# A convolution by two-stage transforms with two MLPs behind it: the last seven rows of the second transform sent from SBUF to SBUF, the inverse of two tiles in one go, two PSUM buffers shared by `ob` and `fk`

## The chip, the cores and the metric

The kernel runs on one core of one Trainium2 chip. The metric is device time in microseconds of one launch. Runs of the kernel before: 1381.61, 1382.43 and 1383.54 us; the median is 1382.43 us.

## What is computed

A gated long convolution over 12480 positions and 128 channels, then two MLPs of width 2048, all in float32:

```python
h_filt = (np.maximum(pos_emb @ w1, 0.0) @ w2) * np.exp(-0.01 * pos)[:, None]
u = x * v                                   # (1, 12480, 128)
y = np.fft.irfft(np.fft.rfft(u, n=L, axis=1) * np.fft.rfft(h_filt, n=L, axis=0), n=L, axis=1)[:, :S]   # L = 2 * S
x = x * y
h = x @ moe_w_in;  x = np.maximum(h, 0.0) ** 2 @ moe_w_out
h = x @ moe2_w_in; out = h / (1.0 + np.exp(-1.702 * h)) @ moe2_w_out
```

## The kernel before, in words

The transform of length 99 x 127 is made of matmuls. A first stage (L291 to L300) multiplies folded inputs by a 99-point table into `A`, 128 partitions by 99 rows (the row index is called k here) by (real, imaginary) by 128 channels.

**The second transform** (`stage_s2`, L322 to L423) goes through the rows in 50 pairs p. Per pair TensorE computes `xk` (spectrum of the signal, L365), every second pair `fk` (features of four filter rows, L342), every fourth pair `hk` (eight filter rows, L357), and two pairs later `ob` (L388), the way back. VectorE multiplies `xk` by the filter into `t` (L374) and subtracts two quarters into half of `P` (L378); GpSimd adds the other half (L377). ScalarE copies `fk`, `hk` and `ob` out of PSUM; the copy of `ob` goes back into `A` in place (L390). `xk` and `hk` have two PSUM buffers each, `fk` one and `ob` one (pool `obp`). Between these VectorE instructions the class `Weights` puts the conversion of MLP weights, which arrive as float64 words: one chunk of 512 columns is eight VectorE instructions on a 128x512 tile (L149, L151, L155, L157, L158, L160, L165, L169) and one ScalarE cast (L167), one step per tick and a tick per pair. Chunks start every six pairs, at pairs 3, 9, ... 45, so that now and then two of them step in the same pair.

Each group of four finished rows is stored from `A` to DRAM (`bd`, L398) and must come back with rows on partitions, because the inverse contracts over rows. For the first four output columns of each half, `load_first` (L490) loads rows 0 to 79, 80 to 87 and 88 to 98 from `bd` into the first columns of `A`; the last three rows are first stored by L394, and the load of the last eleven rows waits for that.

**The junction** between transform and MLPs, in program order: the last `ob` copy on VectorE (L390), the two stores (L394), the loads (L494), the late stores of the remaining columns (L497), `work.finish(EARLY)` with seven ticks of conversion on VectorE, eight combinations of `sums_first` (L455), seven spare matmuls on TensorE (L680), the inverse of tile 0 (20 matmul instructions into one PSUM tile `yps`, L553), the products `hi`, `y`, `lo` (L541 to L543), one more spare matmul, `work.finish()`, and then the MLP loop.

**The MLP loop** (L689 to L723) walks over units: unit (l, t, j) is layer l, tile t of 25 (492 to 502 positions), block j of 256 of the 2048 hidden columns. `unit_in` makes `hin` with six float32r matmuls (high and low parts, L595 to L597), ScalarE applies the activation (two instructions in layer 0), VectorE makes `gh` (`gate`, L636) and `gl` (`low`, L647), and four units later `unit_out` adds six matmuls into `acc`. From unit 40 on layers 0 and 1 alternate. In every tile of layer 0 the next tile is prepared: `load_b` brings two more columns of `bd` (`uv`), `combine_next` adds and subtracts them on VectorE into `b`, `front_y` does the inverse of the next tile on TensorE and multiplies by x on VectorE, `front_x` splits the result. `front_rest` (unit 9) makes the inverse of the two left-over segments into `yr`. The order on every engine is the program's order; nothing is reordered by a scheduler.

The PSUM pool `pms` behind `yps` has two buffers, used in turn:

```python
        pms = es.enter_context(tc.tile_pool(name="pms", bufs=2, space=PSUM, reuse_waits="tile"))
...
        def front_rest():
            ps = pms.tile([D, 512], FP32, tag="m", name="yps")
            inverse(ps, REST)
            nc.vector.tensor_copy(out=yr, in_=ps[:, 0:RESTW])
```

Of the kernel before, what the change touches and what calls it, by code (L numbers as in the profile page):

```python
# [14 lines left out]
ALU = mybir.AluOpType  # L15
# [37 lines left out]
EARLY = 7  # L53
# [19 lines left out]
def widths():  # L73
# [3 lines left out]
    for t, w in enumerate(whole):  # L77
        n = 0
        if t > 1 and left:
            n = min(left, -(-RESTW // (NTILE - 2)))  # L80
            n += (w + n) % 2
            n = left if t == NTILE - 1 else min(n, left)
        rest.append(n)
        left -= n
# [14 lines left out]
def conv_mlp_kernel(ctx: ExitStack, tc: tile.TileContext, xc, xt, vc, pt, w1, w2,  # L99
# [10 lines left out]
    bd = dram.tile([2, NJ, N1, 2, D], FP32, name="bd")  # L110
# [65 lines left out]
    class Weights:  # L176
# [18 lines left out]
        def finish(self, n=1 << 30):  # L195
            while n and (self.run or self.plan):
                self.tick(1 << 30)
                n -= 1
# [123 lines left out]
    def stage_s2(sp, mp, A, w2b, hooks, work):  # L322
# [3 lines left out]
        obp = tc.tile_pool(name="obp", bufs=1, space=PSUM, reuse_waits="tile")  # L326
# [5 lines left out]
        with kp as kp, obp as obp:  # L332
            def features(g):
# [5 lines left out]
                ps = kp.tile([128, FK, 128], FP32, tag="fk", name="fk", bufs=1)  # L339
# [42 lines left out]
            def back(p):  # L382
                n, m, P = pair(p), m_t.pop(p), P_t.pop(p)
                ob = (kp.tile([128, FK, D], FP32, tag="fk", name="ob", bufs=1).rearrange(
                    "p (k c) d -> p k c d", c=2) if p == NP - 2 else
                      obp.tile([128, 2, 2, D], FP32, tag="ob", name="ob"))
# [5 lines left out]
                if p == NP - 1:  # L392
                    for h, queue in ((0, nc.scalar), (1, nc.sync)):
                        queue.dma_start(out=bd[h, 0:JF1, k], in_=A[h * NJ:h * NJ + JF1, k])  # L394
                    for h in range(2):
                        late_h.append((h, k))
                elif k.stop - k.start == HK:
                    nc.scalar.dma_start(out=bd[:, :, k].rearrange("h j k c d -> (h j) k c d"), in_=A[:, k])  # L398
# [29 lines left out]
    def tile_parts(segs):  # L428

        at = 0  # L430
        for j, s, r, n in segs:
            yield j, s, r, n, at
            at += n
# [4 lines left out]
    b_t, x_t, pending = {}, {}, []  # L438
    loaded = [0]
# [6 lines left out]
    def sums(bp, slot):  # L446

        if slot < 2:
            return kept_half(slot)[0:N1].rearrange("p k q -> p (k q)").rearrange(
                "p (j s c d) -> p j s c d", j=JG, s=2, c=2)  # L450
        return bp.tile([N1, JG, 2, 2, D], FP32, tag="b", name="b", bufs=1)
# [16 lines left out]
    def pend(k):  # L468
        pending.extend((k, op) for op in (ALU.add, ALU.subtract))

    def combine_next(n):
        for i in range(min(n, len(pending))):
            combine_two(*pending.pop(0))

    def load_b(bp, t):


        last = max(p[0] for p in whole(t)) // JG
        for k in range(loaded[0], last + 1):
            uv = bp.tile([N1, 2, JG, 2, D], FP32, tag="uv", name="uv", bufs=2)  # L480
            for h in range(2):
                nc.sync.dma_start(out=uv[:, h], in_=bd[h, k * JG:(k + 1) * JG].rearrange("j k c d -> k j c d"))
            b = sums(bp, k % 3)
            b_t[k] = uv, b
            pend(k)
        loaded[0] = last + 1

    late_h = []

    def load_first(A, rows):  # L490


        for h in range(2):
            nc.sync.dma_start(out=A[rows, h * JF1:(h + 1) * JF1],  # L494
                              in_=bd[h, 0:JF1, rows].rearrange("j k c d -> k j c d"))
        for h, k in late_h:
            nc.sync.dma_start(out=bd[h, JF1:NJ, k], in_=A[h * NJ + JF1:(h + 1) * NJ, k])  # L497

    def sums_first(bp, A):
# [392 lines left out]
```

## Time and profile before

| | |
|---|---|
| median of three runs | 1382.43 us |
| the profiled execution | 1382.61 us, of which the span (first to last instruction) is 1380.8 us |
| TensorE busy | 1372.9 us, 99% of the span, 7754 matmul records |
| VectorE busy | 1109.2 us, 80% |
| ScalarE busy | 948.9 us, 69% |
| GpSimd busy | 61.0 us, 4% |
| chain that ended last, by engine | PE 92%, DVE 6%, ScalarE 1%, DMA 1%, issue 1% |
| granted TensorE clock | 0.999 |

PE is TensorE's matmuls, PEld its weight loads, DVE is VectorE, ACT ScalarE, POOL GpSimd, SP the SyncE queue. An instruction with float32 operands stands as two matmul records in the trace. A matmul record's busy time contains its drain, so the time from one start to the next tells the pace (about 0.22 us for 500 columns). The chain of waits goes back from the last instruction, at each step to what released it. In the stage tables the engines stand in the order PE, PEld, DVE, ACT, POOL, and the granted clock behind them is in parts of the full one.

### The profile page before, as it was taken

Reading aid. Unit: us, or ns where it says so; the run is one execution under the profiler, and the core shown is the slowest. Engines: PE = TensorE matmul, PEld = TensorE weight load, DVE = VectorE, ACT = ScalarE, POOL = GpSimd, SP = SyncE. Lnnn points to the kernel's source line nnn. Section 1 sums busy time; section 2 is a strip of 40 time slices with the busy share of each in tenths; the row PEclk is TensorE's granted clock in tenths of the full one; section 3 lists DMA queues with packets and bytes.
Section 4 is the critical chain, followed back from the end, with each engine's and each line's share of the span. In section 5 each row is a group of like instructions: output and inputs, shape, how many; then the busy total and the mean of one; then the engine's idle time right before and its main releaser. Section 6 shows DMA issues by size and latency. Waiting matters only on the chain.

```text
span 1380.8 us, 19037 instructions
## 1 busy us (share of the span) xinstructions
PE 1372.9 (99%) x7754; PEld 1139.9 (83%) x7754; DVE 1109.2 (80%) x1224; ACT 948.9 (69%) x1066; POOL 61.0 (4%) x61
## 2 busy tenths in 40 slices
PE   9999999999999999999999999999999999999998
PEld 8888886888888888888888888888888888888887
DVE  7559998888887787778777887778777887778887
ACT  2655554888776777667767777777777777777776
POOL 3013332000000000000000000000000000000000
PEclk9999999999999999999999999999999999999999
DMA  9968875111210000000000100001000000000000
GB/s 257 306 214 271 270 263 190 55 48 61 70 39 20 15 21 27 20 28 20 27 20 8 40 27 20 8 28 39 20 15 20 28 19 8 9 8 8 9 15 15
DMA packets 45843, 89.25 MB, mean 65 GB/s; under 512 B 4135, under 2 KB 30556, under 8 KB 44988
## 3 DMA queue, kind: packets, MB, share of 16 engines
q1 hardware_dynamic: 36744, 63.33, 15.4%
q10 hardware_dynamic: 9012, 24.70, 4.7%
q8 instruction: 61, 1.00, 0.3%
q14 instruction: 26, 0.21, 0.0%
HBM read 63.21 MB, written 24.81 MB: 64 GB/s over the span
## 4 chain that ended last, share of the span: by engine, by line
PE 92%; DVE 6%; issue 1%; ACT 1%; DMA 1%; SPq 0%; DVEq 0%; ACTq 0%
PE acc L595 13%; PE acc L596 13%; PE acc L597 13%; PE hin L595 13%; PE hin L596 13%; PE hin L597 13%; PE s L295 5%; PE yps L553 3%; DVE t L374 2%; PE ob L388 2%; PE xk L365 2%; PE hk L357 1%; PE fk L342 1%; DVE r L278 1%; DVE words L151 0%
## 5 line engine op out<-in xcount | busy, mean ns | idle before, releaser
L647 DVE TENSOR_TENSOR gl<-g,gh 128x1004 fp32r<-128x1004 f32 (+4 forms) x400 | 477.1, 1193 | 36.9 <-ACT gh L643 36.8
L623 ACT ACTIVATE g<-hin 128x1004 f32<-128x1004 f32 (+4 forms) x200 | 201.0, 1005 | 225.3 <-PE hin L597 219.2
L595 PE MATMUL acc<-gh,w 128*128 128x502 f32 (+4 forms) x800 | 313.8, 392 | 0.6 <-DVE lo L530 0.6
L596 PE MATMUL acc<-gl,w 128*128 128x502 f32 (+4 forms) x800 | 311.4, 389 | 0.6 <-DVE gl L647 0.6
L597 PE MATMUL acc<-gh,w 128*128 128x502 f32 (+4 forms) x800 | 311.4, 389 | 0.0
L595 PE MATMUL hin<-hi,w 128*128 128x502 f32 (+4 forms) x798 | 310.3, 389 | 0.3 <-ACT g L623 0.3
L596 PE MATMUL hin<-lo,w 128*128 128x502 f32 (+4 forms) x798 | 310.5, 389 | 0.0
L597 PE MATMUL hin<-hi,w 128*128 128x502 f32 (+4 forms) x798 | 309.4, 388 | 0.0
L638 DVE TENSOR_TENSOR g<-hin,g 128x1004 f32<-128x1004 f32 (+4 forms) x200 | 238.7, 1194 | 45.7 <-ACT g L628 45.5
L628 ACT ACTIVATE g<-hin 128x1004 f32<-128x1004 f32 (+4 forms) x200 | 200.1, 1000 | 70.4 <-PE hin L597 62.4
L636 DVE CAST gh<-g 128x1004 fp32r<-128x1004 f32 (+4 forms) x185 | 125.8, 680 | 137.1 <-ACT g L624 137.0
L624 ACT ACTIVATE g<-g 128x1004 f32<-128x1004 f32 (+4 forms) x200 | 208.0, 1040 | 6.3
L643 ACT CAST gh<-g 128x1004 fp32r<-128x1004 f32 (+4 forms) x200 | 202.7, 1013 | 0.3 <-DVE g L638 0.3
L595 PEld LDWEIGHTS acc<-gh,w 128*128 128x128 f32 x800 | 150.5, 188 | 33.9 <-DVE lo L530 1.0
L595 PEld LDWEIGHTS hin<-hi,w 128*128 128x128 f32 x798 | 150.2, 188 | 34.1 <-ACT g L623 3.5
L596 PEld LDWEIGHTS acc<-gl,w 128*128 128x128 f32 x800 | 150.9, 189 | 30.4 <-DVE gl L647 1.4
L597 PEld LDWEIGHTS acc<-gh,w 128*128 128x128 f32 x800 | 150.5, 188 | 30.4
L597 PEld LDWEIGHTS hin<-hi,w 128*128 128x128 f32 x798 | 150.4, 188 | 30.4
L596 PEld LDWEIGHTS hin<-lo,w 128*128 128x128 f32 x798 | 150.3, 188 | 30.2
L374 DVE TENSOR_TENSOR t<-xk,hc 128x1024 f32<-128x1024 f32 (+1 forms) x50 | 60.1, 1202 | 11.6 <-ACT hc L359 11.6
L377 POOL TENSOR_TENSOR P<-t 128x256 f32<-128x256 f32 (+1 forms) x50 | 48.4, 968 | 155.4 <-DVE t L374 141.0
L388 PE MATMUL ob<-P,m 128*128 128x256 f32 x198 | 53.0, 391 | 0.3 <-issue 0.3
(79 smaller groups left out, 954.2 us busy)
## 6 DMA issues: line engine op xcount, KB each, us to landing
m<-in_c_s_dram SPq DMA_DIRECT2D x49, 256.0 KB
bd<-A ACTq DMA_DIRECT2D x24, 512.0 KB
uv<-bd SPq DMA_DIRECT2D x62, 198.0 KB
x<-in_xc_dram SPq DMA_DIRECT2D x16, 384.0 KB
v<-in_vc_dram SPq DMA_DIRECT2D x16, 384.0 KB
Gs<-gd ACTq DMA_DIRECT2D x10, 512.0 KB
gd<-G SPq DMA_DIRECT2D x3, 1344.0 KB
pos<-in_pt_dram SPq DMA_DIRECT2D x16, 198.0 KB
```

The source lines that it names most:

```text
L374: nc.vector.tensor_tensor(out=t[:, 0:n], in0=xk[:, 0:n].unsqueeze(3).to_broadcast(full), in1=hc.unsqueeze(2).to_broadcast(full), op=ALU.mult)
L388: nc.tensor.matmul(out=ob[:, j], lhsT=m[:, j, 1, :], rhs=P[:, j])
L595: nc.tensor.matmul(out=out, lhsT=a, rhs=hl[0], start=first, stop=False)
L596: nc.tensor.matmul(out=out, lhsT=a, rhs=hl[1], start=False, stop=False)
L597: nc.tensor.matmul(out=out, lhsT=b, rhs=hl[0], start=False, stop=last)
L623: nc.scalar.activation(out=g, in_=ps, func=ACTF.Relu)
L624: nc.scalar.activation(out=g, in_=g, func=ACTF.Square)
L628: nc.scalar.activation(out=g, in_=ps, func=ACTF.Sigmoid, scale=1.702)
L636: nc.vector.tensor_copy(out=gh, in_=g)
L638: nc.vector.tensor_tensor(out=g, in0=ps, in1=g, op=ALU.mult)
L643: nc.scalar.copy(out=gh, in_=g)
L647: nc.vector.tensor_tensor(out=gl, in0=g, in1=gh.bitcast(FP32), op=ALU.subtract)
```

## The change

It has six parts.

1. `ob` and `fk` take turns on two PSUM buffers of one tag; the pool `obp` is gone. Weight chunks start every seven pairs instead of six, so the eighth and last chunk starts only after the transform.
2. Rows 92 to 98 (`DIRECT`) go from `A` to the load target straight, one DMA of eight pieces of 1 KB per row, on the queues of ScalarE (rows 92, 96, 98) and SP (93, 94, 95, 97). The target is now the ring of `kept` halves instead of `A`. Rows 0 to 83 and 84 to 91 still come over `bd`. `store_late` then stores rows 92 to 98 for all columns in one DMA of 896 KB. `bd` is laid out with the columns of the first tile in front (constant `c_s2` reordered to fit).
3. At the junction five ticks of conversion instead of seven stand in front of the combinations; six combinations instead of eight stand in front of the inverse (the other two behind `lo`). The remaining conversion steps go into units 2 and later, two ticks per unit. Spare matmuls: five in front of the inverse, none behind it.
4. Tile 0's inverse goes into two PSUM tiles: three segments (296 positions) in the first, two (196) in the second; `hi` and `y` are made in two pieces.
5. In every second tile `front_ps` makes the inverse of the next two tiles back to back; `front_rest` moves to unit 19 in front of such a pair. `uv` loads go into the `kept` halves, three `b` buffers.
6. The last unit is split in two halves on ScalarE and VectorE, with its second half of `hin` in a `pms` tile; the last output copy and store are split in two, on two queues.

```diff
-EARLY = 7
+EARLY = 5
+DIRECT = 92
...
+        def go_on(self, n, at=0):
+            for i in range(n):
+                self.tick(at)
...
-                ps = kp.tile([128, FK, 128], FP32, tag="fk", name="fk", bufs=1)
+                ps = kp.tile([128, FK, 128], FP32, tag="fk", name="fk")
...
-                ob = (kp.tile([128, FK, D], FP32, tag="fk", name="ob", bufs=1).rearrange(
-                    "p (k c) d -> p k c d", c=2) if p == NP - 2 else
-                      obp.tile([128, 2, 2, D], FP32, tag="ob", name="ob"))
+                ob = kp.tile([128, FK, D], FP32, tag="fk", name="ob").rearrange("p (k c) d -> p k c d", c=2)
...
+                for i in range(max(2 * p, DIRECT), 2 * p + n):
+                    (nc.scalar if i % 4 == 0 or i == N1 - 1 else nc.sync).dma_start(
+                        out=first_uv()[i:i + 1], in_=A[0:2 * JF1, i])
+                if k.stop - k.start == HK and k.start < DIRECT:
+                    nc.scalar.dma_start(out=bd[:, k], in_=A[:, k])
...
+    def store_late(A):
+        nc.sync.dma_start(out=bd[:, DIRECT:N1], in_=A[:, DIRECT:N1])
...
+        def first_y(ps, x):
...
+            h = inverse(ps[0], whole(0)[0:3])
+            inverse(ps[1], whole(0)[3:], h)
+            parts = (slice(0, h), ps[0]), (slice(h, w), ps[1])
+            for q, p in parts:
+                for o in hi, y:
+                    nc.vector.tensor_tensor(out=o[:, q], in0=p[:, q], in1=x[:, q], op=ALU.mult)
...
-        spare(7)
-        front_y(0)
-        spare(1)
-        work.finish()
+        spare(5)
+        front_first()
...
-        work = Weights([(2, 0), (3, 0), (2, 1), (3, 1)], 6, 12, 4)
+        rest, work = work, Weights([(2, 0), (3, 0), (2, 1), (3, 1)], 10, 10.67, 3)
         for n in range(len(seq) + LAG):
+            rest.go_on(2 * (n > 1), 1 << 30)
...
+                    if lead and j == at:
+                        if t == 2:
+                            front_rest()
+                        front_ps(t + 1)
+                        front_ps(t + 2)
+                        front_y(t + 1)
...
+                    elif lead and j == at + 1:
+                        front_y(t + 2)
...
-            work = Weights([(i, c) for c in range(NWC) for i in range(2)], 3, 6, 5)
+            work = Weights([(i, c) for c in range(NWC) for i in range(2)], 3, 7, 7)
...
+            store_late(A)
+            load_x(lp, 1)
+            work.go_on(EARLY)
+            sums_first(bp)
```

How the order moves on VectorE at the junction. `words` is conversion scratch, `w` the converted weights, `Gs` and `b` the sums, `yps` the inverse in PSUM, `xs` the x tile. Before:

```order
L390 COPY A<-ob 128x256 [waits PE_49]
L151 SCALAR_TENSOR_TENSOR words<-words 128x512
L155 TENSOR_SCALAR words<-words 128x512
L169 TENSOR_TENSOR w_958<-words,w_958 128x512 [waits Activation_49]
L157 TENSOR_SCALAR words<-words 128x512 [waits DVE_49]
L158 TENSOR_SCALAR words<-words 128x512 [waits DVE_49]
L160 SCALAR_TENSOR_TENSOR words<-words 128x512 [waits DVE_49]
L165 SCALAR_TENSOR_TENSOR words<-words 128x512 [waits DVE_49]
L455 TENSOR_TENSOR Gs<-A 99x2x128 [waits DMAHW5_49,DMAHW6_49,DMAHW4_49,DMAHW7_49,DMAHW3_49,DMAHW1_49]
L455 TENSOR_TENSOR Gs<-A 99x2x128 x7
L541 TENSOR_TENSOR hi_2304<-yps,xs 128x492 [waits DMAHW3_49,DMAHW2_49,DMAHW4_49,DMAHW0_49,DMAHW7_49,DVE_49,PE_49]
```

With the change (L-numbers are those of the new file: L152 is old L151, L170 old L169, L156 old L155, L158 old L157, L159 old L158, L161 old L160):

```order
L387 COPY A<-ob 128x256 [waits PE_49]
L152 SCALAR_TENSOR_TENSOR words<-words 128x512
L170 TENSOR_TENSOR w_958<-words,w_958 128x512
L156 TENSOR_SCALAR words<-words 128x512
L158 TENSOR_SCALAR words<-words 128x512 [waits DVE_49]
L159 TENSOR_SCALAR words<-words 128x512 [waits DVE_49]
L161 SCALAR_TENSOR_TENSOR words<-words 128x512 [waits DVE_49]
L463 TENSOR_TENSOR b<-Gs 99x2x128 [waits DMAHW4_49,DMAHW3_49,DMAHW5_49,DMAHW2_49,DMAHW6_49,DMAHW1_49,DMAHW7_49,DMAHW0_49,Pool_49]
L463 TENSOR_TENSOR b<-Gs 99x2x128 x3
L463 TENSOR_TENSOR b<-Gs 99x2x128 [waits Pool_49]
L463 TENSOR_TENSOR b<-Gs 99x2x128
L554 TENSOR_TENSOR hi_2270<-yps,xs 128x296 [waits PE_49]
L554 TENSOR_TENSOR y<-yps,xs 128x296 [waits DMAHW7_49,Activation_49]
```

Six conversion steps are left in front of the first combination, and `hi` starts on 296 positions.

On TensorE the inverse in unit 19, with the change, behind that unit's `hin`: `words` holds the sums of the left-over segments, `b` those of tiles 3 and 4.

```order
L568 MATMUL yps<-ci_61,words 64x98 x8
L568 MATMUL yps<-ci_61,b 64x99 x4
L568 MATMUL yps<-ci_61,b 64x98 x4
L568 MATMUL yps<-ci_61,b 64x99 x4
L568 MATMUL yps<-ci_61,b 64x98 x4
L568 MATMUL yps<-ci_61,b 64x99 x4
L568 MATMUL yps<-ci_61,b 64x98 [waits DVE_49]
L568 MATMUL yps<-ci_61,b 64x98 x3
```

The first row is `front_rest`, the next 20 instructions are tile 3's inverse, and the first of tile 4's waits for VectorE: the third use of two `pms` buffers waits for the copy `yr` of the first. What VectorE has in front of that copy in the program:

```order
L170 TENSOR_TENSOR w_2238<-words,w_2238 128x1024
L538 TENSOR_TENSOR lo_2779<-acc,hi_2778 128x494 [waits Activation_49]
L663 CAST gh<-g 128x2x492 [waits PE_49,Activation_49]
L679 TENSOR_TENSOR gl<-g,gh 128x2x492 [waits DVE_49]
L602 COPY yr<-yps 128x196 [waits PE_49]
```

The `gh` in the third row belongs to unit 19 itself, the `gl` to unit 18. In the kernel before, `front_rest` stood alone in unit 9 and the next `yps` came two units later.

## Rows read from the trace of the kernel before

**Rows 1.** Stage table: stretch, us, busy us (instructions) per engine, clock, DMA share, GB/s

```profile
111.30:133.20 21.90, 21.90 (x162) 19.09 (x162) 20.56 (x26) 11.41 (x17) 7.76 (x8) 1.00 0.78 265
133.20:211.60 78.40, 78.16 (x563) 66.21 (x562) 75.47 (x95) 40.61 (x61) 27.45 (x28) 1.00 0.81 267
235.80:262.00 26.20, 25.81 (x156) 20.77 (x156) 20.94 (x28) 22.49 (x24) 0.00 (x0) 1.00 0.33 106
1377.20:1380.80 3.60, 0.00 (x0) 0.00 (x0) 0.00 (x0) 0.50 (x1) 0.00 (x0) 0.80 0.18 70
```

**Rows 2.** Chain of waits in the second transform: start us, us, what

```profile
116.08 0.87 PE ob L388 x4
...
117.81 0.96 PE ob L388 x4
```

**Rows 3.** Timeline of VectorE in the second transform: start us, us, engine, line, operation

```profile
206.11 1.21 DVE L374 TENSOR_TENSOR t<-xk,hc 128x1024 f32<-128x1024 f32 x1
...
207.76 1.22 DVE L169 TENSOR_TENSOR w<-words,w 128x512 fp32r<-128x512 f32 x1
...
208.90 0.41 DVE L157 TENSOR_SCALAR words<-words 128x512 int32<-128x512 int32 x1
```

**Rows 4.** Chain of waits at the junction

```profile
227.28 1.92 DMA bd<-A
...
230.05 2.03 DMA bd<-A
```

**Rows 5.** Timeline of the junction

```profile
226.57 5.94 PE L680 MATMUL spare<-xs,ci 99*99 99x492 f32 x14
226.78 0.42 DVE L390 COPY A<-ob 128x256 f32<-128x256 f32 x1 [1.10 <-PE ob L388]
...
229.76 0.69 DVE L160 SCALAR_TENSOR_TENSOR words<-words 128x512 int32<-128x512 int32 x1
...
232.10 2.77 DVE L455 TENSOR_TENSOR Gs<-A 99x256 f32<-99x256 f32 x8 [0.92 <-DMA bd<-A]
...
232.58 2.40 PE L553 MATMUL yps<-ci,Gs 99*64 99x99 f32 x40
...
235.03 0.67 DVE L541 TENSOR_TENSOR hi<-yps,xs 128x492 fp32r<-128x492 f32 x1 [0.16 <-PE yps L553]
...
237.04 0.72 PE L613 MATMUL hin<-lo,w 128*128 128x492 f32 x2
```

**Rows 6.** VectorE groups by shape: count, busy us, mean ns

```profile
L566 DVE TENSOR_TENSOR y<-yps,xs 128x490 f32<-128x490 f32 x11 | 7.3, 661 | 0.0
...
L569 DVE TENSOR_TENSOR y<-yr,xs 128x10 f32<-128x10 f32 x14 | 2.2, 159 | 0.0
```

**Rows 7.** Timeline of TensorE around one tile's inverse in the MLP stage

```profile
421.80 0.39 PE L596 MATMUL hin<-lo,w 128*128 128x502 f32 x1
422.03 0.39 PE L597 MATMUL hin<-hi,w 128*128 128x502 f32 x1
...
424.53 0.39 PE L596 MATMUL acc<-gl,w 128*128 128x494 f32 x1
```

**Rows 8.** Chain of waits: the inverse matmuls of that tile, and the first matmuls of all

```profile
3.96 3.56 PE hp L273 x16
...
422.42 1.85 PE yps L553 x40
```

**Rows 9.** Timeline in unit 19 of the MLP stage

```profile
290.39 0.39 PE L597 MATMUL hin<-hi,w 128*128 128x502 f32 x1
...
294.44 1.20 DVE L647 TENSOR_TENSOR gl<-g,gh 128x1004 fp32r<-128x1004 f32 x1
```

**Rows 10.** Timeline of the last unit

```profile
1372.08 1.18 DVE L638 TENSOR_TENSOR g<-hin,g 128x980 f32<-128x980 f32 x1 [0.40 <-ACT g L628]
...
1374.40 0.49 PE L596 MATMUL acc<-gl,w 128*128 128x490 f32 x1 [0.56 <-DVE gl L647]
...
1377.13 0.57 ACT L666 COPY o<-acc 128x490 f32<-128x490 f32 x1 [2.83 <-PE acc L597]
```

More of the change, by code (lines that the diff above doesn't have):

```diff
@@ L78, in widths @@
         n = 0
-        if t > 1 and left:
-            n = min(left, -(-RESTW // (NTILE - 2)))
+        if t > 2 and left:
+            n = min(left, -(-RESTW // (NTILE - 3)))
             n += (w + n) % 2
@@ L330, in pair @@
             return min(2, N1 - 2 * p)
-        with kp as kp, obp as obp:
+        with kp as kp:
             def features(g):
@@ L436, in whole @@
         return WHOLE[SPT * t:SPT * t + SPT]
-    b_t, x_t, pending = {}, {}, []
-    loaded = [0]
+    b_t, x_t, pending, queue, home_of = {}, {}, [], [], {}
+    loaded, loads, first = [0], [0], []
     def load_x(lp, t):
@@ L444, in load_x, with sums, load_uv, first_uv @@
         nc.sync.dma_start(out=x_t[t][:, 0:w], in_=xt[:, STARTS[t]:STARTS[t] + w])
[L446 to L451, printed above, removed]
+    def sums(bp):
+        return bp.tile([N1, JG, 2, 2, D], FP32, tag="b", name="b", bufs=3)
+    def load_uv(k):
+        if loads[0]:
+            uv = kept_half(loads[0] % 2)[0:N1].rearrange("p k q -> p (k q)")
+        else:
+            uv = words(0, 2)[0:N1].bitcast(FP32)
+        uv = uv.rearrange("p (h j c d) -> p h j c d", h=2, j=JG, c=2)
+        loads[0] += 1
+        for h in range(2):
+            j = (JF1, NJ)[h] + k * JG
+            nc.sync.dma_start(out=uv[:, h], in_=bd[j:j + JG].rearrange("j k c d -> k j c d"))
+        return uv
+    def first_uv():
+        return kept[0][0:N1].rearrange("p k q -> p (k q)").rearrange("p (e c d) -> p e c d", e=2 * JF1, c=2)
     def combine(k, s, c):
@@ L488, in conv_mlp_kernel, with load_sum @@
[L488 to L499, printed above, removed]
-        uv = A[0:N1, 0:2 * JF1].rearrange("k (h j) c d -> k h j c d", h=2)
+    def load_sum(bp, k, n):
+        b_t[k] = load_uv(k), home_of.pop(k)() if k in home_of else sums(bp)
+        pending.extend((n, k, op) for op in (ALU.add, ALU.subtract))
@@ new lines, in queue_for, with combine_next, load_next, load_first @@
+    def queue_for(t):
+        last = max(p[0] for p in whole(t)) // JG
+        queue.extend(range(loaded[0], last + 1))
+        loaded[0] = max(loaded[0], last + 1)
+    def combine_next(n, most=1):
+        for i in range(most):
+            if pending and pending[0][0] <= n:
+                combine_two(*pending.pop(0)[1:])
+    def load_next(bp, n):
+        if queue and len({k for _, k, _ in pending}) < 2:
+            load_sum(bp, queue.pop(0), n + 2)
+    def load_first(rows):
+        nc.sync.dma_start(out=first_uv()[rows], in_=bd[0:2 * JF1, rows].rearrange("e k c d -> k e c d"))
@@ L506, in sums_first @@
             for c in range(2):
                 combine(k, s, c)
+        first.extend(sorted({(k, s) for k in range(KF) for s in range(2)} - need))
         loaded[0] = KF
@@ L621, in unit_in @@
             gl = gp.tile([128, 2, MW], F32R, tag="gl", name="gl")[:, :, 0:n]
-            if l == 0:
+            if (l, t, j) == seq[-1]:
+                for c in range(2):
+                    nc.scalar.activation(out=g[:, c], in_=ps[c], func=ACTF.Sigmoid, scale=1.702)
+            elif l == 0:
                 nc.scalar.activation(out=g, in_=ps, func=ACTF.Relu)
@@ L636, in gate @@
                 nc.vector.tensor_copy(out=gh, in_=g)
+            elif (l, t, j) == seq[-1]:
+                for c in range(2):
+                    nc.vector.tensor_tensor(out=g[:, c], in0=ps[c], in1=g[:, c], op=ALU.mult)
             else:
```

151 lines of the change are left out of this document (73 added, 78 removed).

## The prediction

> **What bounds the kernel now.** I read the page's chain of waits first: 92% of it is TensorE, and TensorE is busy 99% of the span at a granted clock of 0.999. So time can only come from places where TensorE waits or does work that the answer does not need. Then I read the span stage by stage and kept the places where the chain leaves TensorE. There are four.
>
> The second transform changes its bound on the way. Work repeats every four pairs. Two such periods early on take 21.90 us, 10.95 each; seven later ones take 78.40 us, 11.20 each, and there VectorE is busy 75.47 of 78.40 us [rows 1]. TensorE's own `ob` matmuls show a step that waits for its single buffer: 0.96 us where the free one takes 0.87 [rows 2]. Inside a late pair, VectorE needs 1.65 us from the start of `t` to the first conversion step behind `P` (206.11 to 207.76) [rows 3].
>
> At the junction nothing but spare matmuls stands on TensorE from 226.57 until the inverse at 232.58. The chain there is DMA: a store of the last rows (1.92 us) and then a load of them (2.03 us), one after the other [rows 4]. VectorE's first combination waits for the load and starts at 232.10, the inverse follows it by 0.48 us, and the first matmul that needs `lo` starts at 237.04 [rows 5].
>
> In the MLP stage TensorE stops briefly wherever it goes from `hin` to an inverse and back [rows 7, 8]. In the last unit it waits for VectorE's `gl`, and the last output copy is 0.57 us [rows 10].
>
> The sum is made against the profiled execution, 1382.61 us; the median of the runs is 1382.43, 0.18 lower, and the last number is shifted by that. A measurement of this kernel tells about 0.2%, 2.8 us, from no change.
>
> **Second transform: -2.5 us (0 to -3.2).** A late pair costs VectorE 11.20 / 4 = 2.80 us; 1.65 is `t` and `P`, so 1.15 is conversion, 6.9 us per chunk at one chunk in six pairs. In seven pairs that is 0.99, a pair 2.64, four pairs 10.56. TensorE's own need is 10.95 less the 0.09 us `ob` stall that two buffers remove, 10.86. So TensorE is the bound again: 7 x (11.20 - 10.86) = 2.4 from the late periods and 5 x 0.09 = 0.5 from the others (50 pairs are some twelve periods). Against it I put 0.4: steps of two chunks still meet in some pairs, and a step is up to 1.14 us (207.76 to 208.90) [rows 3]. If the coupling decides, nothing is gained; with none of it and all twelve periods helped, 3.2. Since 10.56 is well under 10.86 I stay near the full value. `fk` now shares buffers with `ob`, at no cost as long as ScalarE has copied a tile out before the second allocation after it, over half a pair later; without that cover TensorE would stall in every second pair and the gain would be gone.
>
> **Junction: -2.25 us (-1.0 to -2.9).** The `A` copy ends at 227.20 [rows 5]. Row 98 now goes straight to the loads' target. The trace has no such transfer; the nearest row is the store, 1.92 us, and the bounds are half of it and both transfers in a row. At 1.92 it lands at about 229.3. But VectorE still has its first six conversion steps to do, which before ended at 229.76 + 0.69 = 230.45 [rows 5]: so conversion, and no DMA, is the releaser now, and the first combination starts at 230.49 instead of 232.10. Five spares are 10 of 14 records, 5.94 x 10/14 = 4.24 us, and end at 230.81, before the inverse can start (230.49 + 0.48 = 230.97). The inverse takes 2.40 and ends at 233.37. `hi` in two pieces costs one fixed part more: 128x490 takes 661 ns and 128x10 takes 159, so (661 - 159) / 480 = 1.05 ns a column [rows 6]; 296 columns are 0.46 and 196 are 0.35 us, and only the second piece is left when the inverse ends. Two pieces and `lo` behind it bring the first `lo` matmul to about 234.79, 2.25 before 237.04. The two combinations and the spare that are moved behind this point are hidden: TensorE has `hin` to do. The 896 KB store on SP's queue begins while row 98 is under way; if it delays that row by more than 1.2 us, it shows here (the lower bound).
>
> **Pairs of inverses: -2.6 us (-2.3 to -3.2).** From the last `hin` before an inverse to the first `acc` behind it are 2.50 us (422.03 to 424.53) [rows 7]. Of that 0.22 is the `hin` itself (421.80 to 422.03), as much again is lost in the drain, and 1.85 is the inverse [rows 8]: 0.20 is left for changing over. The loop has 25 such stops (24 tiles and the left-over segments); with two tiles at once there are 12. 13 x 0.20 = 2.6. That the second inverse adds no stop of its own is what the order says, except in unit 19.
>
> **A new wait in unit 19: +2.6 us (0 to +3.5).** Left-over segments, tile 3 and tile 4 need three PSUM tiles and there are two. The first matmul of tile 4 waits for `yr`, which VectorE copies only behind a conversion step, `lo`, `gh` and `gl`. In the trace that `gl` starts at 294.44 and takes 1.20 [rows 9]; a copy of 196 columns is 0.35 by the slope above and overlaps the end of `gl` a little, so `yr` is done at about 295.9. TensorE's last `hin` of the unit starts at 290.39 [rows 9] and takes 0.22; the left-over segments are 16 of 40 records, 1.85 x 16/40 = 0.74, tile 3 is 1.85, changing over 0.1: TensorE is ready at 293.3. So it stands 2.6 us. If VectorE runs ahead by that much it stands not at all; if a conversion step more is in front, 3.5. I take the middle reading because this VectorE order is the trace's own, only one conversion step apart. Behind the waiting matmul are tile 4's inverse and `unit_out` of unit 15, and no engine has work that gains by it.
>
> **First units: +0.4 us (0 to +3).** Some ten conversion steps, 5.6 us by the rows of 0.4 to 0.7, move from before the loop into units 2 to 6, where VectorE was busy 20.94 of 26.20 us [rows 1]. 5.3 us of slack for 5.6 of work: it just fits, since `unit_out` asks for `gl` four units late and some 3 us of lag may be used up. Were the lag not there, the whole step cost would show.
>
> **Tail: -0.4 us (0 to -0.9).** VectorE's `g` need not wait 0.40 for the whole activation [rows 10]; a second piece costs 0.1. The output copy in halves on two queues is worth at most half of 0.57, or costs as much in the second transfer.
>
> **Sum:** -2.5 - 2.25 - 2.6 + 2.6 + 0.4 - 0.4 = -4.75; 1382.61 - 4.75 = 1377.86, as a median 1377.7 us.
>
> **The clock, weighed.** At the end of the trace the clock's mean is 0.80 over the 3.6 us in which no matmul runs [rows 1]: at half speed (1.2 of 2.4 GHz) for 1.4 us of these, so it fell about 2.2 us after the last matmul. The pause I expect in unit 19 is 2.6 us, and the change takes away spare matmuls that stand in another. No pause of this length lies inside the span of before, so what a fall costs there is bounded by the first matmuls of all: 16 `hp` records in 3.56 us, 0.22 each [rows 8], about half of that at full clock, which gives up to 1.8 us lost. The Trainium skill, "TensorE: Matmul & The Clock Gate", section "Why this matters for your kernels", says that idle gaps between bursts of matmuls bring the clock back to its lower level, which speaks against this change; the 0.80 agrees that idleness lowers it. By that rule the sum would be 1379.5, by the clock of 0.999 over the span 1377.7.
>
> **The rivals.**
> - *The forecast as it stands* (1375.8 to 1379.2): 45%.
> - *The clock falls in unit 19's pause*: 1377.7 + 1.8 = 1379.5. For it: the 2.2 us; against it: one observation, and the pause may be shorter. 20%.
> - *No pause in unit 19*, because VectorE is ahead there: 1375.1. 10%.
> - *The second transform gains nothing*, since conversion steps of two chunks meet: 1377.7 + 2.5 = 1380.2. 10%.
> - *VectorE becomes the bound in the first units*: the ten steps show on `acc` as waits for `gl`, +2.5 us, 1380.2. Against it: the lag of four units. 8%.
> - *The change does not do what it says at the junction*: the straight rows land late, behind the 896 KB store, and combinations start as before: 1377.7 + 2.25 = about 1379.9. 3%.
> - *Slower*: the same pause in unit 19, but the clock then stays low through the broken-up matmuls behind it. Each us at the lower level costs 0.5. The gain of 4.75 is used up at 9.5 us of low clock, and from about 15 us on the change is slower by over 0.2% (above 1385.2). Against it: it stayed at 1.00 in the stages shown [rows 1]. 4%.
>
> **How the numbers follow.** The forecast, the clock case and the case without a pause hold 75%; the range 1374.2 to 1381.2 takes in the 1380.2 cases too and leaves out the slow one and sums of several bounds. The bound of 0.2% lies at 1379.7: the forecast, the no-pause case and most of the clock case are under it, 71%. The others stay within, 24%; 5% is slower.
>
> **What would show it.** In the changed profile: periods of four late pairs of 10.9 us; the first combination 3.3 us behind the `A` copy, released by VectorE's own conversion; from the last `ob` copy to the first `lo` matmul 7.6 us where it was 9.8; twelve inverses of 80 records; TensorE idle 2.6 us in unit 19 for VectorE's `yr`; the clock still 1.00 behind it; the last `gl` earlier by 0.3. I am wrong if late periods stay at 11.2 us, if TensorE stands still in units 2 to 8, or if the clock shows under 0.95 for the stretch behind unit 19.

## The result, and the profile after

| | before | with the change |
|---|---|---|
| median of 4 runs | 1382.02 us | 1394.16 us (1391.02 to 1394.62) |
| ratio | | 1.0081, 95% interval 1.0064 to 1.0098 |
| profiled execution, span | 1382.61, 1380.8 us | 1394.62, 1392.8 us |
| TensorE busy | 1372.9 us | 1373.5 us |
| mean granted TensorE clock | 0.999 | 0.994 |

The change is slower by 12.1 us, where a median of 1377.7 us was forecast, 4.3 us less than the 1382.02 here: a miss of 16.5 us.

The waits of TensorE, longest first (who waits, for whom, us in total, times, longest):

```profile
PE yps L568 <- DVE yr L602: 3.6, 1, 3.6
PE acc L612 <- DVE w L170: 2.7, 1, 2.7
PE yps L568 <- DVE b L463: 2.4, 1, 2.4
PE acc L611 <- DVE gl L679: 2.1, 4, 1.0
...
PE acc L610 <- DVE lo L538: 0.7, 1, 0.7
```

In the kernel before no wait of TensorE behind the second transform was longer than 0.6 us. Now three are 2.4 to 3.6 us: for `yr` in unit 19 (forecast), for the first combination at the junction and for a conversion step, `w`, at 400 us (neither forecast). The stage table has what stands behind each of the three:

```profile
133.20:211.60 78.40, 78.40 (x592) 69.36 (x591) 75.10 (x91) 41.17 (x62) 28.23 (x29) 1.00 0.80 266
232.40:239.20 6.80, 6.25 (x28) 5.04 (x25) 3.95 (x11) 2.02 (x2) 0.00 (x0) 0.50 0.41 130
297.30:304.00 6.70, 6.07 (x46) 5.40 (x47) 4.27 (x9) 0.00 (x0) 0.00 (x0) 0.50 0.26 61
403.10:406.40 3.30, 3.29 (x8) 2.75 (x9) 2.23 (x3) 0.42 (x1) 0.00 (x0) 0.50 0.02 5
```

In three stretches of 6.8, 6.7 and 3.3 us the granted clock is 0.50, the 1.2 GHz level, and TensorE is busy in all of them; elsewhere it is 1.00, from 7.1 us on and up to the last matmul. A pause so costs twice: its own length, and half of the stretch at half clock. Both matmul pitches stand in the trace: 0.41 us from one `hin` to the next at 237 us, 0.22 us behind 239.2. One of the four executions had a mean clock of 0.998 instead of 0.994, and it is the one with 1391.02 us.

The table follows the executions from landmark to landmark. S2 is from the first `xk` to the end of the last copy into `A`; the other columns count from the end of that copy, to the first combination and to the first activation of a unit on ScalarE (the activations of the trace counted from 0; of 400 units, 398 is the last but one). "Steps" are VectorE's conversion steps between the first combination and unit 9.

| kernel | S2 | comb. | unit 1 | unit 13 | unit 20 | unit 34 | unit 54 | unit 398 | end | steps |
|---|---|---|---|---|---|---|---|---|---|---|
| before | 138.1 | 4.9 | 12.5 | 48.5 | 68.4 | 109.0 | 168.1 | 1141.2 | 1153.6 | 4 |
| the change | 135.6 | 5.6 | 14.8 | 51.1 | 80.9 | 120.0 | 185.2 | 1156.2 | 1168.1 | 10 |
| e1_row98_sp | 135.4 | 3.1 | 10.1 | 48.2 | 79.0 | 118.1 | 183.4 | 1154.2 | 1166.2 | 10 |
| e2_rest_unit17 | 136.0 | 5.6 | 14.6 | 51.3 | 74.9 | 114.0 | 177.6 | 1148.5 | 1160.4 | 10 |
| e3_gap_1066 | 135.4 | 5.6 | 14.6 | 51.1 | 80.9 | 120.0 | 182.5 | 1153.3 | 1165.3 | 10 |
| e4_spare8 | 136.3 | 5.6 | 12.7 | 49.6 | 78.9 | 118.0 | 184.5 | 1155.3 | 1167.2 | 10 |
| e5_all_three | 136.6 | 3.1 | 10.1 | 49.6 | 74.5 | 113.6 | 176.2 | 1147.0 | 1159.1 | 10 |
| e6_gap6 | 137.9 | 3.2 | 10.2 | 43.8 | 67.3 | 106.5 | 167.5 | 1138.3 | 1150.3 | 2 |
| e7_one_buffer | 136.8 | 3.1 | 10.3 | 48.1 | 71.6 | 110.7 | 173.2 | 1144.0 | 1156.0 | 10 |
| e8_first_pair_apart | 135.5 | 3.1 | 10.1 | 48.2 | 72.0 | 111.1 | 172.1 | 1142.8 | 1154.8 | 10 |
| e9_steps_later | 135.7 | 3.1 | 10.2 | 48.1 | 72.2 | 111.3 | 172.3 | 1143.5 | 1155.9 | 10 |
| e11_gap6_start9 | 138.2 | 3.2 | 10.2 | 44.0 | 67.3 | 105.7 | 165.8 | 1136.8 | 1148.7 | 2 |
| e12_gap65 | 136.2 | 2.6 | 9.9 | 46.4 | 70.6 | 109.7 | 170.7 | 1141.6 | 1153.5 | 9 |

Against before, the change gains 2.5 in S2, then loses 2.3 up to unit 1, 10.2 more up to unit 20 and 4.6 more up to unit 54. From there to unit 398 it gains 2.1 and in the tail 0.5. (Up to unit 20 the pairs shift work: the change has done tiles 3 and 4 there, before only tile 3, 1.9 us.)

The timeline of the junction in the changed kernel (start us, us, engine, line, operation, idle before it and releaser):

```profile
224.06 4.29 PE L716 MATMUL spare<-xs,ci 99*99 99x492 f32 x10
224.26 0.42 DVE L387 COPY A<-ob 128x256 f32<-128x256 f32 x1 [1.24 <-PE ob L385]
...
227.18 0.69 DVE L161 SCALAR_TENSOR_TENSOR words<-words 128x512 int32<-128x512 int32 x1
...
230.31 2.10 DVE L463 TENSOR_TENSOR b<-Gs 99x256 f32<-99x256 f32 x6 [2.45 <-DMA words<-bd]
...
230.79 2.92 PE L568 MATMUL yps<-ci,b 99*64 99x99 f32 x40 [2.45 <-DVE b L463]
```

The order is the forecast one: the last copy into `A` ends at 224.68, six conversion steps end at 227.87. But then VectorE stands 2.45 us, the spares are through at 228.35, and the inverse starts at 230.79 (before: 4.9 us from the copy to the first combination, [rows 5]; now 5.6). The releaser's name in that row is only the latest transfer by the profile. The combination waits for all seven rows, and the last of these is late. The transfers of two stretches show it (queue: packets, MB, share of the 16 engines; q1 is SP's queue, q10 ScalarE's). From 226.2 to 229.0:

```profile
q1 hardware_dynamic: 128, 0.92, 100.1%
```

and from 229.0 to 229.2:

```profile
q1 hardware_dynamic: 45, 0.06, 77.6%
q10 hardware_dynamic: 16, 0.01, 13.8%
```

Row 98 is issued on ScalarE's queue as soon as its copy is done, as the 896 KB store is on SP's, both at 225.18. For 2.8 us all 16 engines carry the store's 7 KB packets and nothing else. The 16 packets of row 98, eight of 1 KB with their marks, come at 229.0, and the landings in the trace end at 229.90. The combination starts 0.41 us behind that last landing, here and in the traces of e2, e3 and e4. ScalarE's queue is not slow by itself: row 96 went over it too, issued at 224.44, ahead of the store, and its 16 packets lie between 225.9 and 226.2, 1.5 us behind the issue where row 98's come 3.8 behind theirs:

```profile
q10 hardware_dynamic: 16, 0.01, 15.1%
```

The Trainium skill ("DMA: Bandwidth & Descriptors", section "Queues, rings and completion order") says that an engine takes turns between queues and drains a whole packet, typically some 9 to 17 descriptors, from one before it switches. The profile's packets of 7 KB are the store's single pieces, 128 on 16 engines, so 8 on each: by that rule the store can pass as one turn, and the table of 226.2 to 229.0 agrees. It also says that the mark of a landing is written only behind all earlier writes of that engine, across its queues; with that a row behind the store would land late even if its data had come early, and the landing agrees.

Unit 19 in the changed kernel:

```profile
292.46 1.87 PE L568 MATMUL yps<-ci,b 99*64 99x99 f32 x40
...
296.43 1.17 DVE L679 TENSOR_TENSOR gl<-g,gh 128x984 fp32r<-128x984 f32 x1
297.53 0.35 DVE L602 COPY yr<-yps 128x196 f32<-128x196 f32 x1
...
297.93 3.55 PE L568 MATMUL yps<-ci,b 99*64 99x98 f32 x40 [3.60 <-DVE yr L602]
```

Tile 3's inverse is through at 294.33; `gl` holds VectorE until 297.53, the copy of `yr` follows, and tile 4's inverse starts at 297.93, 3.60 us late. Its 40 matmul records then take 3.55 us where they take 1.87 one row block earlier: the clock was halved at 297.2, still in the pause.

And at 400 us, the second layer's last weights:

```profile
400.05 0.39 PE L611 MATMUL acc<-gl,w 128*128 128x492 f32 x1
...
401.83 1.22 DVE L170 TENSOR_TENSOR w<-words,w 128x1024 fp32r<-128x1024 f32 x1
...
403.11 0.78 PE L612 MATMUL acc<-gh,w 128*128 128x492 f32 x1 [2.67 <-DVE w L170]
```

The matmul of 403.11 reads the converted low words `w`, and their last step stands on VectorE behind `gl`.

What went as forecast is the pairs of inverses (TensorE; the last row is of the kernel before):

```profile
436.59 0.39 PE L612 MATMUL hin<-hi,w 128*128 128x502 f32 x1
436.91 3.61 PE L568 MATMUL yps<-ci,b 99*64 99x99 f32 x80
440.45 0.49 PE L610 MATMUL acc<-gh,w 128*128 128x494 f32 x1
...
424.20 0.49 PE L595 MATMUL acc<-gh,w 128*128 128x494 f32 x1
```

One `hin` takes 0.22 from start to start, so the pair costs 440.45 - 436.59 - 0.22 = 3.64 us. A single tile before took 424.20 - 422.03 - 0.22 = 1.95 (its first `acc` starts at 424.20). And the tail:

```profile
1384.08 1.24 DVE L666 TENSOR_TENSOR g<-hin,g 128x490 f32<-128x490 f32 x2
...
1385.94 0.38 PE L610 MATMUL acc<-gh,w 128*128 128x490 f32 x1
1386.45 0.49 PE L611 MATMUL acc<-gl,w 128*128 128x490 f32 x1
...
1389.20 0.63 ACT L702 COPY o<-acc 128x245 f32<-128x245 f32 x2 [3.24 <-PE acc L612]
```

`g` and the last `gl` work in halves, the `acc` that waits for a `gl` starts 0.51 us behind the matmul before it (0.94 in the kernel before), and the copies of the output are two of 0.3 ([rows 10]: one of 0.57).

### The profile page after: what moved, and what is told of

It reads as the page before. It is cut to its first block, busy times and chain, and to the rows that moved or that the text cites. A ratio compares the mean times of both kernels' runs of the same rounds, so it can differ in the third digit from the quotient of the medians.

```text
span 1392.8 us, 19018 instructions
## 1 busy us (share of the span) xinstructions
PE 1373.5 (99%) x7748; PEld 1146.4 (82%) x7748; DVE 1108.7 (80%) x1228; ACT 948.5 (68%) x1069; POOL 61.0 (4%) x61
## 4 chain that ended last, share of the span: by engine, by line
PE 87%; DVE 8%; ACT 3%; issue 1%; DMA 1%; SPq 0%; DVEq 0%; ACTq 0%
PE acc L610 12%; PE acc L612 12%; PE acc L611 12%; PE hin L610 12%; PE hin L612 12%; PE hin L611 12%; PE s L295 5%; PE ob L385 3%; PE yps L568 3%; PE xk L364 3%; DVE gl L679 3%; PE hk L356 2%; PE fk L341 2%; ACT g L646 1%; ACT g L647 1%
## 5 line engine op out<-in xcount | busy, mean ns | idle before, releaser
L679 DVE TENSOR_TENSOR gl<-g,gh 128x1004 fp32r<-128x1004 f32 (+5 forms) x401 | 476.8, 1190 | 35.3 <-ACT gh L674 35.0
L663 DVE CAST gh<-g 128x1000 fp32r<-128x1000 f32 (+4 forms) x185 | 125.7, 679 | 138.0 <-ACT g L647 138.0
L674 ACT CAST gh<-g 128x1004 fp32r<-128x1004 f32 (+5 forms) x201 | 202.7, 1009 | 0.2 <-DVE g L668 0.2
L568 PEld LDWEIGHTS yps<-ci,b 99*64 99x64 f32 x1000 | 44.8, 141 | 11.4 <-issue 3.9
```

The costliest lines, as they stand in the source:

```text
L568: nc.tensor.matmul(out=ps[d, o:o + w], lhsT=b[:, c, d], rhs=ci2[:, c, r:r + w], start=(c == 0), stop=(c == 1))
L663: nc.vector.tensor_copy(out=gh, in_=g)
L674: nc.scalar.copy(out=gh[:, c], in_=g[:, c])
L679: nc.vector.tensor_tensor(out=gl[:, c], in0=g[:, c], in1=gh.bitcast(FP32)[:, c], op=ALU.subtract)
```

## The experiments

All times are against the kernel before, run on the same chip.

**Row 98 ahead of the store** (e1_row98_sp; on the changed kernel)

```diff
-                    (nc.scalar if i % 4 == 0 or i == N1 - 1 else nc.sync).dma_start(
+                    (nc.scalar if i % 4 == 0 else nc.sync).dma_start(
```

> Row 98 is sent from SP's queue, ahead of the 896 KB store, instead of from ScalarE's. Theory: in the changed kernel row 98's packets start only when the store's are through (229.0 us), the first combination waits for them until 230.31 where VectorE's conversion is done at 227.87, TensorE stands 2.45 us, and the clock is halved from 232.4 to 239.2. Then the first combination now starts about 3.2 us behind the A copy (5.6 before), TensorE does not pause, the clock stays at 1.00 there, and the time falls by 2.4 + 3.0 = 5.4 us to about 1388.8. Rival 1, the clock falls there for another reason: only 2.4 us, 1391.8. Rival 2, row 98 is slow by itself and not because of the store: no change, 1394.2.

Measured 1393.18 us, ratio 1.0075 (1.0060 to 1.0090): 1.0 us less, where 5.4 was expected.

```profile
224.06 0.42 DVE L387 COPY A<-ob 128x256 f32<-128x256 f32 x1 [1.24 <-PE ob L385]
...
226.98 0.69 DVE L161 SCALAR_TENSOR_TENSOR words<-words 128x512 int32<-128x512 int32 x1
...
227.59 2.09 DVE L463 TENSOR_TENSOR b<-Gs 99x256 f32<-99x256 f32 x6
...
234.24 0.69 DVE L472 TENSOR_TENSOR b<-words 99x512 f32<-99x512 f32 x1 [1.73 <-DMA words<-bd]
```

The cause of the late junction is shown, though most of the time that it should give back does not come: row 98 lands at 226.85, 2.4 us behind its copy, the first combination follows the last conversion step with no wait, 3.1 us behind the copy, the clock stays at 1.00, and unit 1 starts 4.7 us earlier than with the change, 2.4 earlier than before. That is the junction's forecast. But of 4.7 only 1.9 are left at unit 20 (79.0 against 80.9): the first units take it back. Over the whole run TensorE now waits for

```profile
PE acc L611 <- DVE gl L679: 3.3, 6, 1.0
...
PE hin L610 <- ACT g L646: 1.7, 2, 1.3
```

of which 2.8 us for `gl` and all of the 1.7 for `g` lie before 290 us, and VectorE waits 1.7 us for a load at 234.24 (its row above). So the first units were a bound behind the first one. That left two candidates, the loads and the steps.

**Left-over segments in unit 17** (e2_rest_unit17; on the changed kernel)

```diff
+                    if t == 2 and j == 1:
+                        front_rest()
                     if lead and j == at:
-                        if t == 2:
-                            front_rest()
                         front_ps(t + 1)
```

> The inverse of the left-over segments moves from unit 19 to unit 17, so that unit 19 needs two PSUM tiles and not three. Theory: TensorE's wait for yr (3.6 us) goes, and with the pause the 6.8 us of half clock behind it (some 3.1 us); one more change between hin and an inverse costs 0.2: 6.5 us less, about 1387.7. Rival 1, the half clock behind unit 19 is not caused by the pause: 3.4 us less, 1390.8. Rival 2, VectorE is behind there whatever waits for it, and TensorE stands the same time a unit later for gl or lo: 1394.2.

Measured 1386.65 us (1384.49 to 1389.54), ratio 1.0032 (1.0020 to 1.0044): 7.5 us less, where 6.5 was expected.

```profile
286.53 0.90 PE L568 MATMUL yps<-ci,words 99*64 99x98 f32 x16
...
292.93 3.62 PE L568 MATMUL yps<-ci,b 99*64 99x99 f32 x80
```

No pause, and 80 records in 3.62 us. Unit 20 comes 6.0 us earlier, and that is what the pause in unit 19 and the half clock behind it cost; another 1.6 us come between units 34 and 54. In this profiled execution the clock did not fall at 400 us either, though the wait for `w` was still 2.7 us: a pause of that length halves the clock in one execution and not in another.

**The last chunk one unit earlier** (e3_gap_1066; on the changed kernel)

```diff
-        rest, work = work, Weights([(2, 0), (3, 0), (2, 1), (3, 1)], 10, 10.67, 3)
+        rest, work = work, Weights([(2, 0), (3, 0), (2, 1), (3, 1)], 10, 10.66, 3)
```

> The distance of the second layer's weight chunks is 10.66 units instead of 10.67, so that the last of the four starts in unit 42 (41.98 rounded up) and not in unit 43 (42.01 rounded up); the other three start where they did. Theory: TensorE's wait of 2.7 us for the last conversion step at 400.4 us, and the 3.4 us of half clock behind it (1.6 us), come from this one unit: 4.3 us less, about 1389.9. Rival, VectorE's load and not the start makes the step late: less than 1 us, 1393.5.

Measured 1390.73 us, ratio 1.0059 (1.0044 to 1.0074): 3.4 us less, where 4.3 was expected. The wait for `w` is gone; another one grows in the units where the chunk now runs:

```profile
PE acc L610 <- DVE lo L538: 1.8, 1, 1.8
```

It was 0.7 with the change, where a conversion step of 0.7 us stood in front of that `lo`; now a step of 1.2 us (behind `gl`) does, and the clock fell behind it for 3.4 us. So the 3.4 us are net of a new pause.

**Eight spares instead of five** (e4_spare8; on the changed kernel; one execution)

```diff
-        spare(5)
+        spare(8)
```

> The changed kernel with eight spare matmuls in front of the first inverse instead of five; row 98 stays on ScalarE's queue. Theory (the clock falls because TensorE pauses): the first combination still stands 5.6 us behind the A copy, but TensorE works until it comes, and the clock stays at 1.00 between 230 and 240; unit 1 starts about 2 us earlier than the 14.8 us behind the A copy of the changed kernel. Rival (the fall has another cause, such as the transfers at that time): half clock for about 6.8 us from 232 as before. Of the total little can be seen, since the first units give most of it back: 1392 to 1394.

Measured 1394.24 us.

```profile
224.59 6.76 PE L716 MATMUL spare<-xs,ci 99*99 99x492 f32 x16
...
230.85 2.10 DVE L463 TENSOR_TENSOR b<-Gs 99x256 f32<-99x256 f32 x6 [2.45 <-DMA words<-bd]
```

```profile
232.40:239.20 6.80, 5.92 (x44) 4.31 (x40) 5.51 (x13) 3.21 (x4) 0.00 (x0) 1.00 0.51 152
```

The wait is the same (5.6 us behind the copy), TensorE works until 231.35, and the stretch that had a clock of 0.50 has 1.00. Unit 1 comes 2.1 us earlier. The store and the loads are the same here, so the pause, and not the transfers, lowers the clock at the junction. It is one execution: the traces of the change, e2 and e3, with the pause, all show the fall, and those of e1, e5 to e9, e11 and e12, without it, do not; but one of e2's six executions has a mean clock of 1.000, so a pause there need not lower it each time. In the total nothing is seen: the stretch at half clock at 400 us is 6.8 us long in this execution, where the change has 3.3.

**All three** (e5_all_three: the edits of e1, e2 and e3)

> Row 98 on SP ahead of the store, the left-over segments in unit 17, and the distance 10.66, all three. Theory, the three places are independent: 5.4 + 6.5 + 4.3 = 16.2 us less than the changed kernel, about 1378.0, and no stretch below 1.00 before the end. Rival, the delays hide one another (a VectorE that starts the loop earlier meets the same conversion steps in units 2 to 6, and waits for gl there grow): about half of the junction's gain is lost again, 1381.

Measured 1381.76 us (1379.94 to 1386.47), ratio 0.9994 (0.9984 to 1.0003). 12.4 of the 16.2 us came, and the rival was near: the junction's gain is lost again in the first units. The profiled execution is the slowest of the ten, so its row stands above those of the next kernels (unit 13 at 49.6, where e8 and e9, with the same steps, have 48.2 and 48.1). Four kernels were made from this one, one for the second transform (e7) and three to find what holds the first units.

**Chunks every six pairs again** (e6_gap6; on e5)

```diff
-            work = Weights([(i, c) for c in range(NWC) for i in range(2)], 3, 7, 7)
+            work = Weights([(i, c) for c in range(NWC) for i in range(2)], 3, 6, 5)
```

> The kernel with all three edits (1381.8 us), but weight chunks start every six pairs again in the second transform, as before the change; what of them is left for the first units is less. Theory: the second transform is held by VectorE's conversion share, so its end comes some 2.4 us later than with seven pairs; and the loss in the first units (unit 13 stands 1.2 us behind the kernel before when both are counted from the A copy, though unit 1 is 2.4 ahead) comes from the conversion steps there, so that it shrinks by up to 3: about 1381.2. Rival 1, the loss in the first units comes from loads that arrive late and not from steps: only the second transform changes, 1384.2. Rival 2, the second PSUM buffer and not the spacing gave the second transform's 2.5 us: its end stays, and the time is between 1378.8 and 1381.8.

Measured 1379.60 us (1378.86 to 1382.32), ratio 0.9984 (0.9975 to 0.9993). S2 is back at 137.9, and the late periods (start to start of `hk`) at up to 11.6 instead of 10.88; the stage table of its late part is the kernel before's for VectorE [rows 1]:

```profile
133.20:211.60 78.40, 77.85 (x560) 66.38 (x558) 75.47 (x95) 40.60 (x61) 27.45 (x28) 1.00 0.79 266
```

Unit 13 comes at 43.8 instead of 48.1 or 48.2 (e8, e9: same steps as e5). So two steps (1.4 us) instead of ten (5.8 us) in the first units are worth 4.3 us there, as much as the eight steps last (4.4), and cost 2.3 in S2.

**One PSUM buffer for `ob`, one for `fk`** (e7_one_buffer; on e5: pool `obp` and `bufs=1` as before the change)

> The kernel with all three edits (1381.8 us), but ob and fk have one PSUM buffer each again; the spacing of seven pairs stays. Theory, as in the prediction: the spacing carries most of the second transform's 2.5 us and the buffers only the stall of 0.09 us in four pairs, 1.1 us over the stage: about 1382.9, with periods of 10.95 us. Rival 1, the buffers carry all of it: 1384.3, periods of 11.2. Rival 2, the buffers carry nothing: 1381.8.

Measured 1383.52 us, ratio 1.0009 (1.0000 to 1.0018): 1.8 us above e5, with periods of 10.97 where the others have 10.88, and S2 at 136.8 where e8 and e9 have 135.5 and 135.7. S2 alone would not settle it, since it is 135.4 to 136.6 in eight traces of the same code up to there (one late period varies from 10.9 to 11.9); the other periods do. The theory holds: the spacing carries most of S2's gain and the buffers about 0.9, 0.09 in each of ten periods, once TensorE is the bound; with chunks every six pairs the buffers alone give next to nothing (e6: 137.9 against 138.1).

**The first pair apart** (e8_first_pair_apart; on e5)

```diff
-                        front_ps(t + 2)
+                        if t:
+                            front_ps(t + 2)
...
-                    elif lead and j == at + 1:
+                    elif t and lead and j == at + 1:
                         front_y(t + 2)
+                    elif t == 0 and j == 6:
+                        front_ps(2)
+                        front_y(2)
```

> The kernel with all three edits (1381.8 us), but the inverses of tiles 1 and 2 stand apart: tile 1 in unit 3, tile 2 in unit 6; the other pairs stay. Theory A: the first units lose time because two tiles' sums are wanted in unit 3, and their loads come from DRAM behind the 896 KB store; VectorE waits for them (3.2 us once) with gates and conversion behind, ScalarE's cast of a weight waits for VectorE, and the next activation waits behind that cast. With tile 2 later, about 2.5 us less, plus 0.25 for one more change: 1379.5. Theory B: the ten conversion steps themselves fill VectorE: no gain, 1382.0.

Measured 1381.25 us, ratio 0.9997 (0.9987 to 1.0006): within the uncertainty of e5. Unit 13 comes at 48.2, as in e1 with the same steps.

**The steps two units later** (e9_steps_later; on e5)

```diff
-            rest.go_on(2 * (n > 1), 1 << 30)
+            rest.go_on(2 * (n > 3), 1 << 30)
```

> The kernel with all three edits (1381.8 us), but the conversion steps that are left start in unit 4 instead of unit 2, at the same two ticks per unit. Theory A (late loads): VectorE stands for the loads all the same, but the cast and the steps no longer lie between the sums and the gates of units 2 and 3: at most 1 us less, 1381. Theory B (the steps fill VectorE): they meet the gates of units 4 to 8 instead and cost the same, 1381.8, or less if VectorE has caught up by then, 1379.8.

Measured 1382.46 us, ratio 0.9999 (0.9990 to 1.0009). Unit 13 at 48.1: unit 2 comes at 13.2 instead of 17.1 (e5), and the steps take that back behind it. TensorE's waits for `gl` are

```profile
PE acc L611 <- DVE gl L679: 3.2, 5, 1.0
```

and in e6

```profile
PE acc L610 <- DVE lo L538: 1.8, 1, 1.8
...
PE acc L611 <- DVE gl L679: 0.6, 2, 0.4
```

Before 290 us the waits for `gl` come to 2.6 us in e9 and to none in e6, and those of `hin` for ScalarE's `g` to 1.1 and 0.3:

```profile
PE acc L611 <- DVE gl L679: 2.6, 3, 1.0
PE hin L610 <- ACT g L646: 1.1, 2, 0.8
```

That is some 3.4 of the 4.3. The wanted second tile (theory A) falls with e8; VectorE's wait for the first load is still 1.6 us in e6 and does not hold it back. The steps (theory B) stand with e6 and e9.

**6.5 pairs** (e12_gap65; on e6: `3, 6.5, 6`)

> The kernel with the three edits, with chunks every 6.5 pairs: between six (1379.6 us, second transform 137.9 us from first xk to A copy, two steps left for the first units) and seven (1381.8 us, 135.6 us, ten steps left). Theory (a step costs VectorE the same wherever it stands, and hides only where TensorE is the bound): the second transform takes some 136.5 us, and the steps left cost in the first units about 0.45 us each; between the two, 1380.5. Rival: the first units can hide half of the steps at no cost, then the middle is better than both ends, 1378.5.

Measured 1380.38 us, ratio 0.9987 (0.9978 to 0.9997): between the two ends. Nine steps are left, and unit 13 comes at 46.4. The seven steps more than in e6 last 3.8 us and cost 2.6 there: no half of them is free, but they do not cost all that they last.

**The second layer's chunks one unit earlier** (e11_gap6_start9; on e6)

```diff
-        rest, work = work, Weights([(2, 0), (3, 0), (2, 1), (3, 1)], 10, 10.66, 3)
+        rest, work = work, Weights([(2, 0), (3, 0), (2, 1), (3, 1)], 9, 10.66, 3)
```

> The kernel with the three edits and chunks every six pairs (1379.6 us), and the second layer's chunks start one unit earlier each. Theory: the wait of 1.8 us for lo in unit 48 comes from two conversion steps of 1.2 us that stand in VectorE's queue in front of it; one unit earlier a shorter step stands there and the wait shrinks by about half a microsecond; with it the half clock that some runs show behind it goes: 1379.0. Rival: the wait has to do with ScalarE's copy or the sums and not with the place of the steps: 1379.6.

Measured 1377.59 us (1376.69 to 1378.11), ratio 0.9965 (0.9953 to 0.9978). The wait for `lo` is

```profile
PE acc L610 <- DVE lo L538: 1.2, 1, 1.2
```

0.6 less than in e6. That is what was expected, and the step in front of `lo` (one, behind `gl`, not two of 1.2 us) is 0.69 us here and 1.22 in e6. The total gained 2.0, of which 0.8 came between units 20 and 34, where other chunks moved too; that part was not tried by itself. This version beats both kernels: 4.5 us less than before.

## Why the prediction was wrong

Five steps held. **Second transform**: -2.5 forecast, 138.1 to 135.6 measured, periods 10.88 (10.9 forecast), and e6 and e7 split it much as the prediction did. **Pairs**: -2.6 forecast; 2 x 1.95 - 3.64 = 0.26 a pair, and from unit 54 to 398, with nine pairs, 2.1. The size was right, its derivation was not: [rows 7] the `acc` at 424.53 is the second one, the first starts at 424.20, and the back-to-back pair itself runs shorter. **Tail**: -0.4, measured 12.4 to 11.9. **The wait in unit 19**: 2.6 forecast with 3.5 as the bound, measured 3.6, just past it, with the very queue in front of `yr` that was named; its size was 1.0 us too small. **The two pieces of `hi`** and what follows the first combination: unit 1 in e1 stands 2.4 us earlier than before, forecast 2.25.

Four steps failed, the third of them unseen in the change itself, and slower by over 0.2% had been given 5%.

- **"At 1.92 it lands at about 229.3 ... so conversion, and no DMA, is the releaser now."** The row landed 5.2 us behind the copy, not 2.1, since it queued behind the 896 KB store. The prediction named this as a rival, gave it 3% and 2.25 us; 1.92 was the time of a 12 KB store that no large one held up: the 512 KB store issued 1.3 us ahead of it had its last packets at 228.1, its own came from 228.2. e1 shows the cause. With the half clock the term was +1.8 at unit 0 instead of -2.25.
- **The clock.** The rival was given 20%, one place and 1.8 us. The price came from 3.56 us of `hp` matmuls at the start, which bound neither how long a half-clock stretch lasts (6.7 and 6.8 us in two of three) nor how often it comes. e4 points to the pause as the cause, and e2 shows that removing one gives 6.0 us by unit 20, where the prediction had 2.6 for the pause alone. The rival *Slower* asked for some 15 us of low clock behind unit 19; there are 6.7 us there and 16.8 in all.
- **First units: "+0.4 ... it just fits."** In the change itself it does: unit 13 starts 36.3 us behind unit 1, in the kernel before 36.0. But that start was late. In e1, with the junction mended, it is 38.1. e6 against e8 and e9: the steps cost there nearly what they last, 4.3 us for eight (e12: 2.6 for seven). The idle time of VectorE in [rows 1] was counted as free, but 5.2 us of it before lie in front of gates that wait for ScalarE's activations, and a step put into the queue delays the `gl` behind it. So, once the junction is mended, the seven-pair spacing moves 4.4 us of steps from a place where they cost 2.3 to one where they cost 4.3.
- **A step that was not costed: `10, 10.67` in place of `6, 12`.** The prediction has no term for it, and so put it at nothing. The last chunk starts at the first unit not below 10 + 3 x 10.67 = 42.01, that is 43, where before it was 6 + 3 x 12 = 42. That one unit is the wait of 2.7 us for `w` at 400 us and the half clock behind it (e3: 3.4 us less, net of a longer wait for `lo`).

From the table: the change against e11 is 14.8 - 10.2 = 4.6 us later at unit 1, 2.5 more by unit 13, 7.2 more by unit 34 and 5.1 more by unit 54, 19.4 in all; its S2 is 2.6 shorter. That is 16.8, against 16.6 between the two medians.

## What to carry to other kernels

Where TensorE is busy 99%, price a pause by its length and by the half-clock stretch behind it, and cover one that can't be removed (the one execution of e4 kept the clock so): three pauses of 2.4 to 3.6 us cost this kernel more than all its gains. Issue a small transfer on the path ahead of a large one that is ready at the same moment; here a queue of its own did not protect it. Work that is moved off a bound stage costs up to its full length wherever its engine's order puts it in front of what the bound engine waits for: read the queue there, not the share of idle time, and round due times by hand before a table of them is changed.

## What the runs showed of the hardware that was not expected

- The clock at the junction fell at 232.4, 1.6 us after TensorE had taken up work again at 230.79, and stayed at 0.50 until 239.2 under steady matmuls. The Trainium skill ("TensorE: Matmul & The Clock Gate", section "Why this matters for your kernels") says that idle gaps between bursts bring the clock back to its lower level; the rows at 0.50 agree, and they show that the fall can come behind the gap.
- A pause of 2.7 us (the wait for `w`) was followed by half clock with the change and not in the profiled execution of e2. Repeats of one kernel lie up to 6.5 us apart (e5: 1379.94 to 1386.47). Of that the trace of the slowest explains 1.7 us by 3.4 us at half clock; the rest lies in S2 and in the first units, and its cause stays open. e11, whose profiled execution shows no half clock before the last matmul, lies within 1.4.
